# Hedgehog linear attention followed by a gated MLP: subtracting the mean inside the normalization instead of negating it first

## The chip, the core and the metric

The kernel runs on one core of one Trainium2 chip. A core has a matrix engine (TensorE, PE in the profile, with its weight loads as PEld), a vector engine (VectorE, DVE), a scalar engine (ScalarE, ACT), a general engine (GpSimd, POOL), and SyncE (SP), which here only issues transfers. Each engine works through its own list of instructions in order and waits on semaphores for the others. The metric is the device time of one execution in microseconds; the time of a kernel is the median of its runs.

## The reference

Two layers run one after the other on 8 batches of 576 positions. The first is an attention with a feature map; the second normalizes half of its hidden features, mixes them over the positions, and multiplies them with the other half. This is the part that the change touches:

```python
def _moe_ref(x, w_in, w_spatial, b_spatial, w_out):
    h = np.maximum(x @ w_in, 0.0)
    d_ff = h.shape[-1]
    u, v = (h[..., :d_ff // 2].copy(), h[..., d_ff // 2:].copy())
    mu = np.mean(v, axis=-1, keepdims=True)
    var = np.mean((v - mu) ** 2, axis=-1, keepdims=True)
    v_n = (v - mu) / np.sqrt(var + 1e-06)
    v_s = np.einsum('ts,bsd->btd', w_spatial, v_n) + b_spatial[None, :, None]
    gated = u * v_s
    return (gated @ w_out).astype(np.float32)
```

Here x is the output of the attention, (8, 576, 512), w_in is 512 x 1024, so u and v have 512 features for each position, w_spatial is 576 x 576 and w_out 512 x 512.

## The kernel before

The order of all work is written out by hand in one long string, ORDER. Each word of it names an operation, its batch and chunk, the PSUM banks or buffers that it takes, and, after an @, the engine (A for ACT, V for DVE, P for POOL, S for SP). Operations of different batches and of the two layers are interleaved there, so that the second layer of one batch runs beside the first layer of later batches. An engine never takes its instructions in another order than the string's: an instruction that waits holds up everything behind it on its engine.

The 576 positions of a batch are four chunks of 128 positions (c = 0 to 3), and a tail of 64. The tails of two batches share the 128 partitions of one tile, so tails go by pairs of batches (g = 0 to 3).

The path of v in the second layer is this, for a chunk of 128 positions by 512 features:

- vm (L964): four matmuls on PE give x times the v half of w_in in a PSUM bank.
- vr: ACT or DVE applies the relu and writes the tile vr, bf16. There are five buffers vr, so a later vr waits until an older one has been read.
- vb and va (L986, L990): DVE gathers mean and variance into mv, a tile that holds the pairs (mean, variance) of two chunks.
- vw (function root): POOL turns two chunks' variances into reciprocal roots in rs. This is done with an addition of 1e-6, a negation of the means in mv, and a power of -0.5.
- vn (function normalize, on POOL): one tensor_scalar with two operations and two scalars per partition, over 128 x 512 elements in bf16, writes the normalized chunk into the tile vn.
- sm (L1046 and L1048 on PE): each output bank takes four matmuls over the four chunks of vn and one over the tail vnt. So the first sm of a batch needs all four vn and the tail.
- sg (L1055 on DVE) multiplies with u, om (L1061 on PE) multiplies with w_out.

The tails have the same steps under the names vmt, vrt, vbt, vat, vwt, vnt and smt (L1113 and L1115 for the matmuls). Where both batches of a pair are done at once, vnt issues two instructions of 64 x 512.

POOL has more to do than this: it scales v by the features' weights in the first layer (vs, vst, L637 and L649), which the matmuls kv (L667, L669) read, divides by the attention's denominator (x, L813), splits the maxima in two bf16 halves (mhl, L682 and L683), and issues some of the loads. All of it stands in the same queue as root and normalize.

In the functions below, [:, :, 0] of mv is the mean and [:, :, 1] the variance; ENG[e] is the engine that the word of ORDER names, which is POOL for every vn and vnt.

Of the kernel before, what the change touches and what calls it, by code (L numbers as in the profile page):

```python
# [11 lines left out]
ALU = mybir.AluOpType  # L12
# [156 lines left out]
def kernel(  # L169
# [16 lines left out]
    nc = tc.nc  # L186
# [47 lines left out]
        mv=([P, 2, 2], FP32),  # L234
        rs=([P, 2, 1], FP32),
# [41 lines left out]
    ENG = dict(A=nc.scalar, V=nc.vector, P=nc.gpsimd, S=nc.sync)  # L277
# [689 lines left out]

    def root(rs, mv, r=slice(0, P)):
        nc.gpsimd.tensor_scalar(out=mv[:, :, 1], in0=mv[:, :, 1], scalar1=1e-6, scalar2=1.0, op0=ALU.add, op1=ALU.mult)
        nc.gpsimd.tensor_scalar(out=mv[:, :, 0], in0=mv[:, :, 0], scalar1=-1.0, scalar2=0.0, op0=ALU.mult, op1=ALU.add)  # L970
        nc.gpsimd.tensor_tensor(out=rs, in0=mv[:, :, 1], in1=neghalf[r, 0:rs.shape[1]], op=ALU.pow)

    def normalize(e, out_, in_, mv, rs):
        ENG[e].tensor_scalar(out=out_, in0=in_, scalar1=mv, scalar2=rs, op0=ALU.add, op1=ALU.mult)  # L974

    @op
    def vm(e, b, c):
# [14 lines left out]
    @op  # L992
    def vw(e, b, cc):
        root(get("rs", (b, cc)).rearrange("p n o -> p (n o)"), at["mv", (b, cc)])

    @op
    def vn(e, b, c):
        cc, y = c // 2, c % 2
        normalize(e, get("vn", b)[:, c, 0:HALF], at["vr", (b, c)], at["mv", (b, cc)][:, y, 0:1], at["rs", (b, cc)][:, y, :])
# [17 lines left out]
    @op  # L1017
    def vwt(e, g, i):
        root(get("rs", ("t", g, i))[rows[i], 0, :], at["mv", ("t", g, i)][rows[i], 0:1, :], rows[i])

    @op
    def vnt(e, g, i):
        for bl in parts[i]:
            r = rows[bl]
            normalize(e, get("vnt", g)[r, bl, :], at["vr", ("t", g, i)][r], at["mv", ("t", g, i)][r, 0, 0:1],
                      at["rs", ("t", g, i)][r, 0, :])
# [114 lines left out]
    with tc.manual_schedule():  # L1141
        for word in ORDER.split():
            word, _, e = word.partition("@")
# [35 lines left out]
```

## Time and profile before

| what | value |
|---|---|
| time, median of 3 runs | 258.3 us (257.01 to 259.43) |
| span of the profiled execution, first to last instruction | 253.3 us |
| median less the span | 5.0 us |
| busy: PE / DVE / ACT / POOL | 242.0 / 216.3 / 202.6 / 194.3 us |
| normalizing instructions (L974) on POOL | 40, 24.4 + 6.2 us busy |
| negations (L970) on POOL | 21, 4.1 us busy |
| granted TensorE clock over the span | 1.000 |

The profile is of one execution. The page does not list that execution's own total time; its span is 253.3 us, and the 5.0 us between span and median stand for what lies around it. Groups of instructions are given as their line, engine, operation, tiles and shapes, then the number of instructions, busy microseconds, mean nanoseconds of one, and how long the engine idled ahead of them and for whom. In the timeline a row is one instruction, or several alike, with its start, its length from the first start to the last end, and the idle time ahead in square brackets. A few matmul records are missing from the trace, so a group of four can read x3.

### The profile page before, as it was taken

Reading aid. Unit: us, or ns where it says so; the run is one execution under the profiler, and the core shown is the slowest. Engines: PE = TensorE matmul, PEld = TensorE weight load, DVE = VectorE, ACT = ScalarE, POOL = GpSimd, SP = SyncE. Lnnn points to the kernel's source line nnn. Section 1 sums busy time; section 2 is a strip of 40 time slices with the busy share of each in tenths; the row PEclk is TensorE's granted clock in tenths of the full one; section 3 lists DMA queues with packets and bytes.
Section 4 is the critical chain, followed back from the end, with each engine's and each line's share of the span. In section 5 each row is a group of like instructions: output and inputs, shape, how many; then the busy total and the mean of one; then the engine's idle time right before and its main releaser. Section 6 shows DMA issues by size and latency. Waiting matters only on the chain.

```text
span 253.3 us, 8099 instructions
## 1 busy us (share of the span) xinstructions
PE 242.0 (96%) x3254; PEld 155.5 (61%) x3291; DVE 216.3 (85%) x374; ACT 202.6 (80%) x344; POOL 194.3 (77%) x312
## 2 busy tenths in 40 slices
PE   7999989999999999898999999999999999999993
PEld 7888778656656666665565576556446765644542
DVE  1899989999999978999999999999998979657540
ACT  4899889999989999999999999889989702434222
POOL 8369997999698898589989996999899833495400
PEclk9999999999999999999999999999999999999999
DMA  7999995999899998999999969897730260521145
GB/s 197 304 184 254 234 245 91 195 145 126 165 282 113 122 265 131 208 225 154 171 180 256 196 149 207 89 256 183 228 113 15 44 123 6 208 44 41 52 113 208
DMA packets 80089, 41.33 MB, mean 163 GB/s; under 512 B 48946, under 2 KB 75442, under 8 KB 80052
## 3 DMA queue, kind: packets, MB, share of 16 engines
q1 hardware_dynamic: 58772, 30.06, 50.7%
q0 software_dynamic: 20592, 10.10, 32.3%
q10 hardware_dynamic: 688, 0.66, 0.8%
q8 instruction: 25, 0.41, 0.7%
q14 instruction: 12, 0.10, 0.1%
HBM read 32.82 MB, written 9.44 MB: 167 GB/s over the span
## 4 chain that ended last, share of the span: by engine, by line
PE 73%; DMA 7%; POOL 6%; DVE 6%; ACT 4%; issue 3%; SPq 0%; POOLq 0%; DVEq 0%
PE banks L1032 11%; PE banks L964 10%; PE banks L1061 10%; PE banks L1046 9%; PE banks L582 5%; DMA ld<-in_q_dram 5%; PE banks L667 4%; PE banks L790 3%; PE banks L369 3%; DMA xT<-x 2%; PE banks L513 2%; POOL vs L637 2%; PE banks L762 2%; PE banks L1048 2%; DVE mq L587 2%
## 5 line engine op out<-in xcount | busy, mean ns | idle before, releaser
L712 ACT ACTIVATE qf<-banks 128x1024 bf16<-128x1024 f32 x72 | 70.8, 1033 | 2.1 <-PE banks L697 0.7
L637 POOL TENSOR_TENSOR vs<-v,em 128x512 bf16<-128x512 f32 x64 | 65.6, 1043 | 2.5 <-PE banks L697 1.8
L591 ACT ACTIVATE kf<-banks 128x1024 bf16<-128x1024 f32 x64 | 63.3, 1037 | 2.7 <-PE banks L582 1.9
L587 DVE TENSOR_REDUCE mq<-banks 128x8 f32<-128x1024 f32 x36 | 43.2, 1214 | 1.4 <-PE banks L582 0.9
L587 DVE TENSOR_REDUCE mk<-banks 128x8 f32<-128x1024 f32 x32 | 38.6, 1215 | 1.6 <-PE banks L582 1.5
L1032 PE MATMUL banks<-xT,w_u 128*128 128x512 bf16 x128 | 32.3, 379 | 0.4 <-DVE mq L587 0.3
L1046 PE MATMUL banks<-w_spT,vn 128*128 128x512 bf16 x117 | 31.8, 379 | 0.5
L964 PE MATMUL banks<-w_v,xT 128*128 128x512 bf16 x115 | 30.4, 379 | 1.3 <-DMA xT<-x 0.5
L1061 PE MATMUL banks<-w_out,uT 128*128 128x512 bf16 x115 | 29.4, 379 | 0.6 <-issue 0.2
L1055 DVE TENSOR_TENSOR uT<-banks,uT 128x512 bf16<-128x512 f32 x32 | 21.7, 682 | 6.4 <-PE banks L1048 3.8
L281 ACT COPY ob<-banks 128x512 f32<-128x512 f32 (+1 forms) x24 | 14.0, 582 | 15.9 <-PE banks L1061 13.5
L813 POOL TENSOR_TENSOR x<-tq,rc 128x512 bf16<-128x512 f32 x16 | 16.7, 1044 | 12.7 <-DVE rc L810 9.6
L974 POOL TENSOR_SCALAR vn<-vr,mv,rs 128x512 bf16<-128x512 bf16 x32 | 24.4, 769 | 1.2
L986 DVE BATCH_NORM_STATS2 st<-vr 128x6 f32<-128x512 bf16 x32 | 21.5, 680 | 3.6 <-ACT vr L287 3.3
L667 PEld LDWEIGHTS <-kf 128*128 128x128 bf16 x512 | 21.9, 97 | 4.3 <-issue 0.4
L667 PE MATMUL banks<-vs,kf 128*128 128x66 bf16 x512 | 24.4, 194 | 0.0
L582 PE MATMUL banks<-wphi,T 64*128 64x128 bf16 x512 | 22.9, 217 | 0.4 <-ACT uT L287 0.3
L669 PE MATMUL banks<-vst,kft 128*128 128x66 bf16 x128 | 21.2, 192 | 0.0
L582 PEld LDWEIGHTS <-T 64*128 64x128 bf16 x512 | 15.9, 94 | 8.4 <-issue 6.4
L1032 PEld LDWEIGHTS <-w_u 128*128 128x128 bf16 x128 | 11.4, 97 | 12.8 <-issue 1.2
L287 ACT ACTIVATE vr<-banks 128x512 bf16<-128x512 f32 (+1 forms) x23 | 13.7, 604 | 6.1 <-POOL vnt L974 3.4
L1046 PEld LDWEIGHTS <-vn 128*128 128x128 bf16 x128 | 11.4, 97 | 11.5
(137 smaller groups left out, 512.1 us busy)
## 6 DMA issues: line engine op xcount, KB each, us to landing
v<-in_v_dram SPq DMA_DIRECT2D x16, 512.0 KB, 6.1
out_dram<-ob SPq DMA_DIRECT2D x31, 256.0 KB, 2.7
ld<-in_k_dram POOLq DMA_DIRECT2D x7, 512.0 KB, 8.8
ld<-in_q_dram POOLq DMA_DIRECT2D x7, 512.0 KB, 8.1
out_dram<-ob SPq DMA_DIRECT2D x9, 128.0 KB, 4.7
uT<-in_q_dram SPq DMA_DIRECT2D x2, 512.0 KB, 6.3
vt<-in_v_dram SPq DMA_DIRECT2D x8, 128.0 KB, 3.3
vn<-in_moe_w_spatial_dram POOLq DMA_DIRECT2D x1, 576.0 KB, 8.1
```

The costliest lines, as they stand in the source:

```text
L582: nc.tensor.matmul(out=bank(banks[y])[:, n * F:(n + 1) * F], lhsT=xT[halves[y], n, :], rhs=wphi[halves[y], :], start=True, stop=True)
L587: nc.vector.tensor_reduce(out=out_, in_=pp.rearrange("p y (n f) -> p y n f", f=F), axis=AX.X, op=ALU.max, apply_absolute_value=True)
L591: nc.scalar.activation(out=kf[:, s].rearrange("p y n f -> p y (n f)"), in_=pp, func=AF.Exp, bias=0.0, scale=(1.0, -1.0)[s])
L637: ENG[e].tensor_tensor(out=get("vs", (b, j))[:, s, :, 0:D], in0=at["v", (b, j // 2)][:, (j % 2) * n:(j % 2 + 1) * n, :], in1=at["em", (b, ...
L667: nc.tensor.matmul(out=pv[:, hh, s, :], lhsT=kf[:, s, c % 2, 2 * hh + c // 2, :], rhs=w[:, s, NB * hh + c, :], start=(c == 0), stop=False)
L712: nc.scalar.activation(out=at["qf", u][:, s].rearrange("p y n t -> p y (n t)"), in_=at["pq", u], func=AF.Exp, bias=0.0, scale=(1.0, -1.0)[s])
L964: nc.tensor.matmul(out=bank(place)[r], lhsT=lhs[:, kc, r], rhs=w_v[:, kc, :], start=(kc == 0), stop=(kc == KC - 1))
L974: ENG[e].tensor_scalar(out=out_, in0=in_, scalar1=mv, scalar2=rs, op0=ALU.add, op1=ALU.mult)
L1032: nc.tensor.matmul(out=bank(place).rearrange("p (c t) -> p c t", c=NB), lhsT=w_u[:, kc, dc * P:(dc + 1) * P], rhs=at["xT", b][:, :, kc, :] ...
L1046: nc.tensor.matmul(out=bank(place), lhsT=at["vn", b][:, c, cs], rhs=w_spT[:, c, 0:T0], start=(c == 0), stop=False)
L1055: nc.vector.tensor_tensor(out=u, in0=at["psp", (b, dc)], in1=u, op=ALU.mult)
L1061: nc.tensor.matmul(out=bank(place), lhsT=at["uT", b][:, dc, c * P:(c + 1) * P], rhs=w_out[:, dc, :], start=(dc == 0), stop=(dc == KC - 1))
```

## The change

The function root no longer multiplies the means by -1, and normalize subtracts the mean as its first operation where it added the negated mean. Its second operation, the multiplication by rs, stays.

```diff
     def root(rs, mv, r=slice(0, P)):
         nc.gpsimd.tensor_scalar(out=mv[:, :, 1], in0=mv[:, :, 1], scalar1=1e-6, scalar2=1.0, op0=ALU.add, op1=ALU.mult)
-        nc.gpsimd.tensor_scalar(out=mv[:, :, 0], in0=mv[:, :, 0], scalar1=-1.0, scalar2=0.0, op0=ALU.mult, op1=ALU.add)
         nc.gpsimd.tensor_tensor(out=rs, in0=mv[:, :, 1], in1=neghalf[r, 0:rs.shape[1]], op=ALU.pow)
 
     def normalize(e, out_, in_, mv, rs):
-        ENG[e].tensor_scalar(out=out_, in0=in_, scalar1=mv, scalar2=rs, op0=ALU.add, op1=ALU.mult)
+        ENG[e].tensor_scalar(out=out_, in0=in_, scalar1=mv, scalar2=rs, op0=ALU.subtract, op1=ALU.mult)
```

ORDER is the same, and the lists of the other engines are the same but for the line numbers behind L970, which are one lower. On POOL, 21 rows go. This is the place in POOL's list where the first batch is normalized for the first time: mv_150 holds two chunks' means and variances, rs_156 their reciprocal roots.

```order
 L969 TENSOR_SCALAR mv_150<-mv_150 128x2
-L970 TENSOR_SCALAR mv_150<-mv_150 128x2
-L971 TENSOR_TENSOR rs_156<-mv_150,neghalf 128x2
+L970 TENSOR_TENSOR rs_156<-mv_150,neghalf 128x2
 L402 DMA ld_62<-in_k_dram 128x8x256
```

Between the addition (L969) and the power (L971 before, L970 now) nothing is left. In the second batch the same piece, with the numbers of the buffers and the semaphores that an instruction waits for in brackets (Pool is POOL's own), reads:

```order
 L969 TENSOR_SCALAR mv_5_155<-mv_5_155 128x2 [waits DVE_49]
-L970 TENSOR_SCALAR mv_5_155<-mv_5_155 128x2
-L971 TENSOR_TENSOR rs_4_160<-mv_5_155,neghalf_179 128x2 [waits Pool_49]
-L974 TENSOR_SCALAR vn_2_163<-vr_2_143,mv_5_155,rs_4_160 128x512 [waits Pool_49]
+L970 TENSOR_TENSOR rs_4_160<-mv_5_155,neghalf_179 128x2 [waits Pool_49]
+L973 TENSOR_SCALAR vn_2_163<-vr_2_143,mv_5_155,rs_4_160 128x512 [waits Pool_49]
```

The power waits for POOL's own addition in both, and the normalization waits for the power; the negation had waited for nothing. The normalizations keep their places, tiles and shapes; only their first operation differs, which the rows do not show.

## Prediction

> **What bounds the kernel now.** I read the page first, for the busy shares of the engines.
>
> ```profile
> span 253.3 us, 8099 instructions
> PE 242.0 (96%) x3254; PEld 155.5 (61%) x3291; DVE 216.3 (85%) x374; ACT 202.6 (80%) x344; POOL 194.3 (77%) x312
> POOL 8369997999698898589989996999899833495400
> ```
>
> PE is busy for 96% of the span, so the kernel ends when PE's list ends, and a change counts by the idle time that it puts into PE or takes out. Only 11.3 us (253.3 less 242.0) could be taken out at all. POOL's row in 40 slices of 6.3 us says that its 77% is an average: between slice 8 and slice 32 it is mostly at 8 or 9 tenths. What POOL does later there, it does later for everything behind it.
>
> Then the groups of POOL's instructions, shapes kept apart, for what the touched instructions cost and for other instructions of the same size.
>
> ```profile
> L637 POOL TENSOR_TENSOR vs<-v,em 128x512 bf16<-128x512 f32 x64 | 65.6, 1043 | 2.5 <-PE banks L697 1.8 <-ACT em L596 0.2
> L974 POOL TENSOR_SCALAR vn<-vr,mv,rs 128x512 bf16<-128x512 bf16 x32 | 24.4, 769 | 1.2
> L974 POOL TENSOR_SCALAR vnt<-vr,mv,rs 64x512 bf16<-64x512 bf16 x8 | 6.2, 769 | 0.4
> L971 POOL TENSOR_TENSOR rs<-mv,neghalf 128x2 f32<-128x2 f32 x16 | 11.2, 701 | 0.0
> L683 POOL TENSOR_TENSOR mhl<-mq,mhl 128x8 bf16<-128x8 f32 x19 | 3.8, 202 | 1.6
> L970 POOL TENSOR_SCALAR mv<-mv 128x2 f32<-128x2 f32 x16 | 3.1, 193 | 1.3
> L969 POOL TENSOR_SCALAR mv<-mv 128x2 f32<-128x2 f32 x16 | 3.1, 193 | 5.8 <-DVE mv L990 4.8
> L337 POOL TENSOR_SCALAR sel<-sel 128x512 bf16<-128x512 bf16 x1 | 1.5, 1517 | 0.0
> L283 POOL COPY vnt<-ident 128x512 bf16<-128x512 bf16 x2 | 1.2, 612 | 0.0
> ```
>
> The time of an instruction on POOL depends on the arithmetic as well as on the size: a power over 2 elements per partition (L971) takes 701 ns, a subtraction over 8 (L683) 202 ns. And two tensor_scalar instructions of one size and type differ by a factor of two: L974, an addition followed by a multiplication, takes 769 ns; L337, which multiplies by -1 with no second operation, takes 1517 ns.
>
> Last the timeline, at the places where normalized chunks are handed to PE: the last normalizations of each of the eight batches on POOL, and the matmuls that read them.
>
> ```profile
> 60.08 3.02 POOL L974 TENSOR_SCALAR vn<-vr,mv,rs 128x512 bf16<-128x512 bf16 x4
> 63.09 0.76 POOL L974 TENSOR_SCALAR vnt<-vr,mv,rs 64x512 bf16<-64x512 bf16 x1
> 86.59 2.28 POOL L974 TENSOR_SCALAR vn<-vr,mv,rs 128x512 bf16<-128x512 bf16 x3
> 131.35 1.63 POOL L974 TENSOR_SCALAR vnt<-vr,mv,rs 64x512 bf16<-64x512 bf16 x2
> 141.64 1.53 POOL L974 TENSOR_SCALAR vn<-vr,mv,rs 128x512 bf16<-128x512 bf16 x2
> 180.26 1.63 POOL L974 TENSOR_SCALAR vnt<-vr,mv,rs 64x512 bf16<-64x512 bf16 x2
> 191.96 1.53 POOL L974 TENSOR_SCALAR vn<-vr,mv,rs 128x512 bf16<-128x512 bf16 x2
> 228.41 0.77 POOL L974 TENSOR_SCALAR vn<-vr,mv,rs 128x512 bf16<-128x512 bf16 x1
> 234.43 3.03 POOL L974 TENSOR_SCALAR vn<-vr,mv,rs 128x512 bf16<-128x512 bf16 x4
> ...
> 64.89 0.38 PE L1048 MATMUL banks<-w_spT,vnt 128*128 128x512 bf16 x1
> 88.72 1.02 PE L1046 MATMUL banks<-w_spT,vn 128*128 128x512 bf16 x3
> 133.46 0.38 PE L1048 MATMUL banks<-w_spT,vnt 128*128 128x512 bf16 x1
> 146.05 0.28 PE L1113 MATMUL banks<-w_spT,vn 128*128 128x64 bf16 x4
> 182.86 0.38 PE L1048 MATMUL banks<-w_spT,vnt 128*128 128x512 bf16 x1
> 193.74 0.81 PE L1046 MATMUL banks<-w_spT,vn 128*128 128x512 bf16 x3
> 229.70 0.81 PE L1046 MATMUL banks<-w_spT,vn 128*128 128x512 bf16 x3
> 238.91 0.28 PE L1113 MATMUL banks<-w_spT,vn 128*128 128x64 bf16 x4
> ```
>
> POOL's end (start plus length) against PE's start gives the slack of each hand-over: batch 0, 64.89 - 63.85 = 1.04 us; batch 1, the last chunk is read by the last matmul of the group, which starts at 88.72 + 1.02 - 0.38 = 89.36, so 89.36 - 88.87 = 0.5; batch 2, 133.46 - 132.98 = 0.5; batch 3, 146.05 - 143.17 = 2.9; batch 4, 182.86 - 181.89 = 1.0; batch 5, 193.74 - 193.49 = 0.25; batch 6, 229.70 - 229.18 = 0.5; batch 7, 238.91 - 237.46 = 1.45. PE does not wait for POOL here, but in six of eight batches it arrives within about 1 us of it.
>
> **The change part by part.** The first part takes 21 negations out of POOL's list. Starts tell what each holds up; the rows of the first root, and a pair beside it whose second instruction waits for the first:
>
> ```profile
> 55.19 0.19 POOL L969 TENSOR_SCALAR mv<-mv 128x2 f32<-128x2 f32 x1
> 55.46 0.19 POOL L970 TENSOR_SCALAR mv<-mv 128x2 f32<-128x2 f32 x1
> 55.62 0.73 POOL L971 TENSOR_TENSOR rs<-mv,neghalf 128x2 f32<-128x2 f32 x1
> 57.31 0.21 POOL L682 CAST mhl<-mq 128x8 bf16<-128x8 f32 x1
> 57.60 0.20 POOL L683 TENSOR_TENSOR mhl<-mq,mhl 128x8 bf16<-128x8 f32 x1
> ```
>
> From the addition's start to the power's start are now 55.62 - 55.19 = 0.43 us. With the negation gone the power follows the addition whose result it needs; the row of that kind nearest by is L682 to L683, 0.29 us, and L969 to L970 is 0.27. I take 0.27, so a root gets 0.16 us shorter, and the 21 together 3.4 us. The Trainium skill (Perfetto Trace Analysis, GPSIMD Engine Instruction) says that a GpSimd instruction's recorded span is unreliable and should be replaced by the spacing of starts; by that rule the trace agrees, since L970's span is 0.19 us where the next start comes 0.16 us later. By spans the sum would be 21 x 0.193 = 4.1 us instead.
>
> The second part changes the first operation of 40 normalizations (32 vn, 8 vnt) from an addition to a subtraction. The trace shows no tensor_scalar on POOL that subtracts, so its price is bounded by the rows of the same size. Below stands the COPY with 612 ns, a pass without arithmetic; the price of an addition, 769, lies just above. L637, two tensors read, takes 1043. L337 takes 1517 with one operation; if a second operation cost as much again beyond the 193 ns that a small tensor_scalar takes (L970), that would be 1517 + 1324 = 2841 ns. I take 1517 ns. Every tensor_scalar on POOL that is an addition and a multiplication, in either order, belongs to the cheap kind as far as its size lets one see (L974, 769; L969 and L970 are too small to tell); the only one that is something else, L337, costs double. Its input is one column repeated, but so is that of the COPY, which is the faster of all, so the reading is not what makes it slow. A subtraction with a multiplication is something else as well; that it shares L337's price is my choice.
>
> At 1517 ns a normalization takes e = 0.748 us longer. On POOL this is 40 x 0.748 - 3.4 = +26.5 us, of 194.3. What PE sees is worked out batch by batch: normalizations times e, less roots times 0.16, plus what POOL still lags from before, less POOL's idle ahead, less the slack above. After a hand-over that stalls PE, the schedule as a whole is later, and POOL lags it by the slack; where POOL then idles, that lag goes.
>
> - Batch 0: 5 normalizations, 3 roots: 3.74 - 0.48 = 3.26, less 1.04: PE stalls 2.2 us.
> - Batch 1: its tail and first chunk with their roots add 1.18, of which POOL's idle of 0.34 takes some; one root and three chunks add 2.08; 2.92 less 0.5: 2.4.
> - Batch 2: three chunks and two roots add 1.92, an idle of 0.80 takes some; one root, a chunk and two tails add 2.08; 3.2 less 0.5: 2.7.
> - Batch 3: 4 normalizations, 2 roots: 2.67, with a lag of 0.5, less 2.9: 0.3.
> - Batch 4: 6 normalizations, 3 roots: 4.0, less 1.0: 3.0.
> - Batch 5: 2.67, a lag of 1.0 less an idle of 0.29, less 0.25: 3.1.
> - Batch 6: the first chunk is lost in an idle of 2.50; 5 normalizations, 2 roots: 3.4, less 0.5: 2.9.
> - Batch 7: 2.67, less 1.45: 1.2.
>
> The idle times are these:
>
> ```profile
> 85.36 0.19 POOL L969 TENSOR_SCALAR mv<-mv 128x2 f32<-128x2 f32 x1 [0.34 <-DVE mv L990]
> 127.58 0.19 POOL L969 TENSOR_SCALAR mv<-mv 128x1 f32<-128x1 f32 x1 [0.80 <-DVE mv L1015]
> 182.19 0.19 POOL L969 TENSOR_SCALAR mv<-mv 128x2 f32<-128x2 f32 x1 [0.29 <-DVE mv L990]
> 221.73 1.04 POOL L813 TENSOR_TENSOR x<-tq,rc 128x512 bf16<-128x512 f32 x1 [2.50 <-DVE rc L810]
> ```
>
> The sum is 17.8 us. Against the profiled execution the span would be 253.3 + 17.8 = 271.1, and with the 5.0 us around it 276.1: the forecast is 276 us. What queues behind a slower normalization on POOL (vs, x, mhl, loads) is late by the same lag; I count it only through PE's stall, which is the weak point of the sum: where the chunk's slack is large, as in batch 3, a late vs or x may stall PE in its place. The Trainium skill (GPSIMD Engine Reference, Performance pitfalls for Q7 kernels) has a dependent chain of fp32 operations at 4 cycles an element unless it is unrolled; at the 1.2 GHz that the page gives, an estimate from it for 512 elements is 1.71 us, and the same eight lines would give 25 us and 284. No row here shows cycles, and L974 with 769 ns is faster than such a chain.
>
> **The rivals.** The first is that a subtraction costs what an addition costs: then nothing but the negations changes. For it speaks L683, where a subtraction of two tensors takes 0.20 us beside the 0.21 us of the conversion L682 ahead of it; against it L337. The place is L974 at 769 ns, and the point from which it decides is a price below about 0.85 us, where 40 x 0.08 = 3.2 us undo the 3.4 us of the roots. PE waits nowhere for a normalization now, so it gains little; at most the 0.16 us of one to three roots in the three tightest batches, some 0.5 us, gives 257.8 us, not slower. The lower bound of 612 ns would take another 6.3 us off POOL, and no more than 1.5 us off PE: 256.5. [...]
>
> The second is that both operations are priced like L337's one, 2841 ns. Then e is 2.07, POOL's work is 40 x 2.07 - 3.4 = 79 us more, 274 us in all, and POOL becomes the bound: the eight lines give 8.8, 9.0, 10.6, 5.6, 10.9, 8.4, 9.5 and 6.5, together 69 us, and 328 us.
>
> The third is a mild price, that of L637, 1043 ns: e is 0.274, batches 0, 3 and 7 hide theirs, and 0.2, 0.2, 0.2, 1.2 and 0.5 remain: 2.3 us, and 260.6.
>
> **How the numbers follow.** I give the forecast, a price from 1.25 to 2.1 us, 0.47; the same price as an addition 0.28; the mild price 0.10; a price above 2.1 us 0.15. The forecast's own range is 267 (1.25 us: 8 us by the same lines) to 300 us (2.1 us: 41 us). The range of 8 in 10 has to take in the first rival, which reaches from 256.5 to 259, and leaves out the prices above 2.1 us and a few hundredths below 257: 257 to 300. A measurement of this kernel can tell about 1%, 2.6 us, from no change. Faster by more than that is left only to the lower bound, 0.04; within 1% are the rest of the first rival and half of the mild price, 0.28; slower is 0.68.
>
> **What would show it.** In the profile of the changed kernel the normalization's group (line 973) shows the price at once: near 1500 ns for the forecast, 769 for the first rival, near 2800 for the second. The start of the power should come 0.27 us after the addition's. If the price is near 1500 ns, PE should idle ahead of L1045 and L1047 (before L1046 and L1048) for 2 to 3 us in batches 0, 1, 2, 4, 5 and 6 and hardly in batch 3. The prediction is wrong in its price if the group reads otherwise, and in its sum if the group reads 1500 ns and the time is not within some 5 us of 276: then POOL's lag reached PE through vs and x, or was lost in idle time that I counted as fixed.

## The result, and the profile after

The changed kernel takes 304.7 us (median of 6 runs, 303.2 to 306.3) against 256.5 us for the kernel before in the same comparison: a ratio of 1.188 (95% interval 1.184 to 1.193). That is 48 us slower, where 18 us slower and 276 us were forecast, and it lies above the range of 257 to 300.

The page of the changed kernel, its busy shares and the chain that ended last:

```profile
span 301.6 us, 8078 instructions
PE 255.9 (85%) x3254; PEld 159.6 (53%) x3291; DVE 217.6 (72%) x374; ACT 203.4 (67%) x344; POOL 243.2 (81%) x291
POOL 48%; PE 28%; DVE 9%; issue 6%; DMA 5%; POOLq 1%; ACT 1%; SPq 0%; DVEq 0%
```

The span grew by 48.3 us, POOL's busy time by 48.9 us (194.3 to 243.2). POOL now makes up 48% of the chain, with PE at 28%. PE, which was busy for 96% of the span, is busy for 85%; and its own busy time grew by 13.9 us though it has the same matmuls: its mean granted clock was 0.949 in this execution, against 1.000 before.

POOL's groups, shapes kept apart, and the longest waits for POOL:

```profile
L973 POOL TENSOR_SCALAR vn<-vr,mv,rs 128x512 bf16<-128x512 bf16 x32 | 66.2, 2074 | 1.2
L973 POOL TENSOR_SCALAR vnt<-vr,mv,rs 64x512 bf16<-64x512 bf16 x8 | 16.6, 2073 | 0.4
L970 POOL TENSOR_TENSOR rs<-mv,neghalf 128x2 f32<-128x2 f32 x16 | 11.4, 714 | 1.3
L337 POOL TENSOR_SCALAR sel<-sel 128x512 bf16<-128x512 bf16 x1 | 1.5, 1522 | 0.0
...
PE banks L1045 <- POOL vn L973: 16.7, 6, 5.8
DVE tq L802 <- POOL x L813: 11.7, 5, 4.2
```

A normalization takes 2074 ns where it took 769: 40 x 1.305 = 52 us more. L337 is where it was. PE, which waited nowhere for a normalization before, waits 16.7 us for them ahead of L1045 (and 4.0 us ahead of L1047 and L1112), and DVE waits 11.7 us for the division x, which stands in the same queue.

The first root in the timeline:

```profile
54.95 0.19 POOL L969 TENSOR_SCALAR mv<-mv 128x2 f32<-128x2 f32 x1
55.23 0.73 POOL L970 TENSOR_TENSOR rs<-mv,neghalf 128x2 f32<-128x2 f32 x1
```

From the addition to the power are 0.28 us, 0.27 by the prediction, against 0.43 before. So the part that removes the negations did on POOL what was expected.

For each batch, the first matmul that reads its normalized tail (sm, or smt for batches 3 and 7), in the trace of before and then of after:

```profile
64.89 0.38 PE L1048 MATMUL banks<-w_spT,vnt 128*128 128x512 bf16 x1
89.58 0.38 PE L1048 MATMUL banks<-w_spT,vnt 128*128 128x512 bf16 x1
146.16 0.19 PE L1115 MATMUL banks<-w_spT,vnt 128*128 128x64 bf16 x1
194.39 0.38 PE L1048 MATMUL banks<-w_spT,vnt 128*128 128x512 bf16 x1
230.56 0.38 PE L1048 MATMUL banks<-w_spT,vnt 128*128 128x512 bf16 x1
239.03 0.19 PE L1115 MATMUL banks<-w_spT,vnt 128*128 128x64 bf16 x1
```

```profile
69.76 0.61 PE L1047 MATMUL banks<-w_spT,vnt 128*128 128x512 bf16 x1 [0.59 <-POOL vnt L973]
100.99 0.63 PE L1047 MATMUL banks<-w_spT,vnt 128*128 128x512 bf16 x1
151.32 0.39 PE L1047 MATMUL banks<-w_spT,vnt 128*128 128x512 bf16 x1 [1.24 <-POOL vnt L973]
168.46 0.19 PE L1114 MATMUL banks<-w_spT,vnt 128*128 128x64 bf16 x1
212.47 0.63 PE L1047 MATMUL banks<-w_spT,vnt 128*128 128x512 bf16 x1
231.98 0.63 PE L1047 MATMUL banks<-w_spT,vnt 128*128 128x512 bf16 x1
276.58 0.63 PE L1047 MATMUL banks<-w_spT,vnt 128*128 128x512 bf16 x1 [0.22 <-issue]
287.31 0.19 PE L1114 MATMUL banks<-w_spT,vnt 128*128 128x64 bf16 x1
```

(Batches 2 and 4 of before, at 133.46 and 182.86, stand in the prediction.) The difference at a batch, less the difference at the batch before it, is the delay that the batch adds. Beside it stands what the eight lines of the prediction give with the measured price, e = 2.074 - 0.769 = 1.305 us, in place of 0.748:

| batch | 0 | 1 | 2 | 3 | 4 | 5 | 6 | 7 | sum |
|---|---|---|---|---|---|---|---|---|---|
| lines, at 2.07 us | 5.0 | 5.2 | 6.1 | 2.5 | 6.4 | 5.4 | 5.7 | 3.5 | 39.8 |
| after | 4.9 | 6.5 | 6.4 | 4.4 | 7.3 | 8.0 | 8.4 | 2.3 | 48.3 |

(The lines' entries are rounded; unrounded they sum to 39.6.) The first batch is on the line; from then on every batch but the last adds 0.3 to 2.7 us more. Another thing in these rows: in five of eight the matmul is recorded with 0.61 to 0.63 us where 0.38 is usual.

So two questions were left: why a subtraction costs 2.07 us and not 1.52, and where the 8.7 us beyond the lines come from.

### The profile page after: what moved, and what is told of

The parts are those of the page before. It is cut to its first block, busy times and chain, and to the rows that moved or that the text cites. A ratio compares the mean times of both kernels' runs of the same rounds, so it can differ in the third digit from the quotient of the medians.

```text
span 301.6 us, 8078 instructions
## 1 busy us (share of the span) xinstructions
PE 255.9 (85%) x3254; PEld 159.6 (53%) x3291; DVE 217.6 (72%) x374; ACT 203.4 (67%) x344; POOL 243.2 (81%) x291
## 4 chain that ended last, share of the span: by engine, by line
POOL 48%; PE 28%; DVE 9%; issue 6%; DMA 5%; POOLq 1%; ACT 1%; SPq 0%; DVEq 0%
POOL vn L973 19%; POOL vs L637 8%; PE banks L1045 6%; POOL vnt L973 5%; POOL rs L970 5%; DMA ld<-in_q_dram 4%; PE banks L369 3%; POOL x L813 2%; PE banks L1060 2%; PE banks L582 2%; PE banks L513 2%; DVE mq L587 2%; PE banks L667 2%; POOL vst L649 2%; DVE tq L802 2%
## 5 line engine op out<-in xcount | busy, mean ns | idle before, releaser
L973 POOL TENSOR_SCALAR vn<-vr,mv,rs 128x512 bf16<-128x512 bf16 x32 | 66.2, 2074 | 1.2
L1045 PE MATMUL banks<-w_spT,vn 128*128 128x512 bf16 x117 | 38.7, 443 | 20.2 <-POOL vn L973 16.7
L1045 PEld LDWEIGHTS <-vn 128*128 128x128 bf16 x128 | 12.5, 108 | 35.3 <-POOL vn L973 18.2
L813 POOL TENSOR_TENSOR x<-tq,rc 128x512 bf16<-128x512 f32 x16 | 16.7, 1043 | 13.9 <-DVE rc L810 11.0
L802 DVE TENSOR_TENSOR tq<-banks,wq 128x528 f32<-128x528 f32 x17 | 12.0, 704 | 16.7 <-POOL x L813 11.7
L287 ACT ACTIVATE uT<-banks 128x512 bf16<-128x512 f32 x23 | 13.8, 609 | 15.1 <-PE banks L1031 14.9
## 6 DMA issues: line engine op xcount, KB each, us to landing
out_dram<-ob SPq DMA_DIRECT2D x31, 256.0 KB, 2.7
```

Source lines behind the costliest of these rows:

```text
L287: nc.scalar.activation(out=out_, in_=in_, func=AF.Relu, bias=0.0, scale=1.0)
L1045: nc.tensor.matmul(out=bank(place), lhsT=at["vn", b][:, c, cs], rhs=w_spT[:, c, 0:T0], start=(c == 0), stop=False)
```

## The experiments

### Prices of eleven pairs of operations

```diff
+        scr = [buf["vr"][3], buf["xt"][0].rearrange("p h d -> p (h d)")]
+        vin, m1, r1 = at["vr", (7, 3)], at["mv", (7, 1)][:, 1, 0:1], at["rs", (7, 1)][:, 1, :]
+        pairs = [(ALU.add, ALU.mult), (ALU.subtract, ALU.mult), (ALU.mult, ALU.add), (ALU.mult, ALU.subtract),
+                 (ALU.add, ALU.add), (ALU.subtract, ALU.add), (ALU.mult, ALU.mult), (ALU.max, ALU.mult),
+                 (ALU.add, None), (ALU.subtract, None), (ALU.mult, None)]
+        for i, (a, c) in enumerate(pairs):
+            nc.gpsimd.tensor_scalar(out=scr[i % 2], in0=vin, scalar1=m1, scalar2=None if c is None else r1, op0=a,
+                                    **({} if c is None else dict(op1=c)))
```

> The kernel before, with eleven more tensor_scalar instructions on GpSimd behind its last one, all over the same 128 x 512 bf16 tile with the same two scalars per partition, one for each pair of operations: add-mult, subtract-mult, mult-add, mult-subtract, add-add, subtract-add, mult-mult, max-mult, and add, subtract and mult alone. Their results go nowhere. Theory (the price hangs on the pair of operations, a few pairs being cheap): add-mult 770 ns, subtract-mult 2070 ns, mult alone about 1520 ns, mult-add cheap as well. Rival (the price hangs on the place or on contention in the changed kernel): subtract-mult 770 ns here, where nothing else runs on GpSimd.

The timeline of POOL behind its last normalization, in the order of the list in the diff:

```profile
238.08 0.78 POOL L1156 TENSOR_SCALAR vr<-vr,mv,rs 128x512 bf16<-128x512 bf16 x1
238.83 2.10 POOL L1156 TENSOR_SCALAR xt<-vr,mv,rs 128x512 bf16<-128x512 bf16 x1
240.91 0.78 POOL L1156 TENSOR_SCALAR vr<-vr,mv,rs 128x512 bf16<-128x512 bf16 x1
241.66 2.10 POOL L1156 TENSOR_SCALAR xt<-vr,mv,rs 128x512 bf16<-128x512 bf16 x1
243.73 2.11 POOL L1156 TENSOR_SCALAR vr<-vr,mv,rs 128x512 bf16<-128x512 bf16 x1
245.81 2.10 POOL L1156 TENSOR_SCALAR xt<-vr,mv,rs 128x512 bf16<-128x512 bf16 x1
247.87 0.79 POOL L1156 TENSOR_SCALAR vr<-vr,mv,rs 128x512 bf16<-128x512 bf16 x1
248.62 2.11 POOL L1156 TENSOR_SCALAR xt<-vr,mv,rs 128x512 bf16<-128x512 bf16 x1
250.69 1.59 POOL L1156 TENSOR_SCALAR vr<-vr,mv 128x512 bf16<-128x512 bf16 x1
252.24 1.59 POOL L1156 TENSOR_SCALAR xt<-vr,mv 128x512 bf16<-128x512 bf16 x1
253.78 1.59 POOL L1156 TENSOR_SCALAR vr<-vr,mv 128x512 bf16<-128x512 bf16 x1
```

Add-mult, mult-add and mult-mult take 0.78 to 0.79 us. Subtract-mult, mult-subtract, add-add, subtract-add and max-mult take 2.10 to 2.11 us, and each operation alone, addition and multiplication among them, takes 1.59 us. So the price hangs on the pair as a whole, not on the subtraction: an addition after an addition is as dear. The results go to the tiles xt and vr in turn; a single operation takes 1.59 us into either. Nothing else runs on POOL here, and DVE is idle from 246.3 to 250.3 us while the prices stay the same, so contention is not the reason.

### Sizes, fixed numbers, and VectorE

```diff
+        for a, c, n in [(ALU.add, ALU.mult, 128), (ALU.add, ALU.mult, 256), (ALU.subtract, ALU.mult, 128),
+                        (ALU.subtract, ALU.mult, 256)]:
+            nc.gpsimd.tensor_scalar(out=scr[0][:, 0:n], in0=vin[:, 0:n], scalar1=m1, scalar2=r1, op0=a, op1=c)
+        for a, c in [(ALU.add, ALU.mult), (ALU.subtract, ALU.mult)]:
+            nc.gpsimd.tensor_scalar(out=scr[0], in0=vin, scalar1=0.5, scalar2=2.0, op0=a, op1=c)
...
+            nc.vector.tensor_scalar(out=scr[1], in0=vin, scalar1=0.5, scalar2=2.0, op0=a, op1=c)
...
+            nc.vector.tensor_scalar(out=scr[1], in0=vin, scalar1=m1, scalar2=r1, op0=a, op1=c)
```

> The kernel before, with more instructions behind GpSimd's last one. On GpSimd: add-mult and subtract-mult over 128 and 256 columns, then both over 512 columns with fixed numbers in place of the scalars per partition. On VectorE: both pairs over 512 columns, with fixed numbers and with scalars per partition. Theory (a slow path of GpSimd for every pair but a few, with a price per element): from 2.07 us at 512 columns and some 0.2 us fixed, subtract-mult takes 0.67 us at 128 and 1.14 us at 256 columns, add-mult 0.34 and 0.48; fixed numbers change nothing; VectorE takes the same time for both pairs. Rival (a fixed price of 1.3 us for each slow instruction, code that has to be found): subtract-mult 1.6 us at 128 columns.

Each line's own durations (least, median and greatest, in ns), and the two sizes of the first line apart:

```profile
L1155 POOL TENSOR_SCALAR vr<-vr,mv,rs x4: 462/684/1222, 237.6 to 239.7; 128x128 bf16<-128x128 bf16 x2, 128x256 bf16<-128x256 bf16 x2
L1157 POOL TENSOR_SCALAR vr<-vr x2: 619/1272/1924, 241.0 to 241.7; 128x512 bf16<-128x512 bf16 x2
L1161 DVE TENSOR_SCALAR xt<-vr,mv,rs x2: 412/412/412, 250.8 to 251.3; 128x512 bf16<-128x512 bf16 x2
...
L1155 POOL TENSOR_SCALAR vr<-vr,mv,rs 128x256 bf16<-128x256 bf16 x2 | 1.8, 890 | 0.2
L1155 POOL TENSOR_SCALAR vr<-vr,mv,rs 128x128 bf16<-128x128 bf16 x2 | 1.3, 636 | 0.1
```

The pairs of means give add-mult 462 and 558 ns at 128 and 256 columns, and subtract-mult 810 and 1222 ns. With 769 and 2074 at 512 columns, add-mult grows by 0.75 to 0.82 ns a column, subtract-mult by 3.2 to 3.3, from the same fixed part of some 0.4 us. The rival of a fixed price falls. The expected 0.34, 0.48, 0.67 and 1.14 us were all some 0.1 us low, since the fixed part had been taken from small instructions without scalars per partition; fixed numbers save 0.15 us for either pair (0.62 and 1.92 us), which had been expected to change nothing. On VectorE both pairs take 412 ns: the price belongs to GpSimd.

### The two parts of the change alone

```diff
-        nc.gpsimd.tensor_scalar(out=mv[:, :, 0], in0=mv[:, :, 0], scalar1=-1.0, scalar2=0.0, op0=ALU.mult, op1=ALU.add)
```

> The first part of the change alone: the 21 negations go, the normalization keeps its addition. (It then adds the mean where it should subtract it.) Theory: GpSimd's list gets 21 x 0.16 = 3.4 us shorter, PE waits nowhere for it, so the time stays within 1 us of the kernel before, 256 to 257 us. Rival (the root's power now stalls behind the addition): 21 x 0.1 us or more of lost time, 258 us or more.

Measured: 255.98 us, a ratio of 0.995 (0.991 to 0.999). The change without its dear pair of operations is a small gain, 1.3 us (0.2 to 2.4), where no more than 1 us was expected; the rival's loss of time behind the addition did not come.

```diff
-        ENG[e].tensor_scalar(out=out_, in0=in_, scalar1=mv, scalar2=rs, op0=ALU.add, op1=ALU.mult)
+        ENG[e].tensor_scalar(out=out_, in0=in_, scalar1=mv, scalar2=rs, op0=ALU.subtract, op1=ALU.mult)
```

> The second part of the change alone: the normalization subtracts, and the 21 negations stay. (It then adds the mean.) Theory (GpSimd's list now sets the time at nearly every hand-over): the negations cost all of their 21 x 0.16 = 3.4 us, so 3 to 4 us more than the changed kernel, about 308 us. Rival (they are hidden as in the kernel before): within 1 us of the changed kernel, 304 to 305.5 us.

Measured: 307.3 us, a ratio of 1.199 (1.195 to 1.204), 2.6 us more than the changed kernel. So the second part makes the whole loss. By the intervals of the two ratios the 2.6 us are uncertain by some 1.6 us. So the rival's 1 us is unlikely, and most of POOL's list is on the path now, as the theory has it; whether all of it is, 2.6 against 3.4 us, cannot be told.

### The forecast's own price

```diff
-        ENG[e].tensor_scalar(out=out_, in0=in_, scalar1=mv, scalar2=rs, op0=ALU.add, op1=ALU.mult)
+        ENG[e].tensor_scalar(out=out_, in0=in_, scalar1=rs, scalar2=None, op0=ALU.mult)
```

(This is against the kernel before; the negation L970 goes as well.)

> The normalization at the forecast's own price: no negation, and one multiplication by rs with no second operation. (The mean is not subtracted at all.) Price expected 1520 ns. The eight lines of the prediction give 17.8 us, so 256.5 + 17.8 = 274 us. If the lines miss something that grows with the stalls, as the 48 us of the changed kernel against 40 by the lines at 2.07 us suggest, 276 to 280 us.

Measured: 281.7 us, a ratio of 1.094 (1.087 to 1.102), more than either expectation, with this group:

```profile
L973 POOL TENSOR_SCALAR vn<-vr,rs 128x512 bf16<-128x512 bf16 x32 | 49.9, 1568 | 1.1
```

At 1568 ns, e is 0.80 us and the lines give 19.9 us. Measured are 24 us (0.094 x 257.3), again some 4 us more. So the lines are short by about a fifth of what is measured at both prices: what they lack grows with the stalls.

### The clock behind the stalls

The matmuls of 0.61 us after a wait pointed to TensorE's clock. This was tried by keeping PE busy while it waits:

```diff
-sm.0.0:0
+warm.60:0 sm.0.0:0
-sm.1.0:3
+warm.45:3 sm.1.0:3
-sm.4.2:5
+warm.45:5 sm.4.2:5
-sm.5.1:2
+warm.45:2 sm.5.1:2
-sm.6.0:5
+warm.90:5 sm.6.0:5
```

> The changed kernel with small matmuls on the identity put ahead of the first sm of batches 0, 1, 4, 5 and 6 (60, 45, 45, 45, 90 of them, into the bank that this sm fills next), so that PE is busy for most of the time in which it waits for the normalization. Their results are overwritten. Theory (the stalls of 3 us and more bring a lower clock behind them, which is the part of the 48 us that the lines lack): the mean granted clock goes from 0.95 to 0.98 or more and the time falls by 4 to 9 us, to 296 to 301 us. Rival (the rest is lag that reaches PE through vs, x and their buffers): the time stays at 304 us or grows.

Measured: 300.75 us, a ratio of 1.167 (1.158 to 1.176), a mean granted clock of 0.971: 4 us less than the changed kernel, at the end of what was expected, with a clock below the 0.98 expected. At batch 4 this kernel was 31.8 us behind the kernel before, where the changed one was 29.6 (its first tail matmul starts at 214.68 against 212.47). There the small matmuls filled no wait:

```profile
208.63 4.96 PE L369 MATMUL banks<-ident 128*128 128x128 bf16 x45 [2.98 <-ACT vr L287]
```

They write the bank that ACT's relu vr has to empty first, and this vr had itself waited 3.40 us for POOL to read an older tile vr. So they start only after the wait of 2.98 us. The granted clock was 1.00 up to 206 us and 0.50 from 208 us on, and the 45 took 4.96 us, where they take 2.67 at batch 1 below. (In the changed kernel the first sm of batch 4 waits 2.97 us for the same vr, a path from POOL to PE that the lines do not have.) They were left out there in the next run:

> The changed kernel with the small matmuls ahead of the first sm of batches 0, 1, 5 and 6 only (60, 45, 45, 90); those ahead of batch 4 are left out, since the run with five places lost some 6 us there. Theory (the lower clock behind long stalls is a good part of what the lines lack): mean granted clock 0.98 or more, 294 to 299 us. Rival (the gain of the first such run was chance, or lost again at the next hand-over, because GpSimd's list sets the time): 301 us or more.

Measured: 298.85 us, a ratio of 1.165 (1.160 to 1.171), granted clock 0.980 against 0.949. The 5.9 us less (uncertain by some 1.8 us) came as the theory expected. They are what the small matmuls save, not all that the lower clock costs, for the clock is not back at 1.000. At batch 1 it is seen best. These are windows of 11 us around its hand-over, in the changed kernel and then in this one, and the window around batch 2's in the changed kernel; after the busy times of the engines stands the granted clock:

```profile
96.00:107.00 11.00, 7.66 (x69) 4.11 (x72) 3.71 (x8) 4.40 (x10) 8.92 (x10) 0.69 0.43 104
```

```profile
94.00:105.00 11.00, 9.55 (x135) 6.31 (x134) 5.65 (x11) 6.47 (x13) 10.68 (x11) 1.00 0.39 98
```

```profile
150.00:165.00 15.00, 11.65 (x141) 6.47 (x143) 10.63 (x20) 11.81 (x23) 14.27 (x14) 1.00 1.17 204
```

And the matmuls at batch 1 without and with the small ones ahead:

```profile
98.53 0.61 PE L1045 MATMUL banks<-w_spT,vn 128*128 128x512 bf16 x1 [2.70 <-POOL vn L973]
101.41 1.91 PE L1045 MATMUL banks<-w_spT,vn 128*128 128x512 bf16 x4
```

```profile
93.66 2.67 PE L369 MATMUL banks<-ident 128*128 128x128 bf16 x45
99.05 1.03 PE L1045 MATMUL banks<-w_spT,vn 128*128 128x512 bf16 x4
```

In the changed kernel the granted clock is 1.00 up to 98.0 us and 0.50 from 98.25 to 104.75 us. The first matmul after 2.70 us without work takes 0.61 us, and four later ones take 1.91; with 45 small ones put into that wait the four take 1.03. Around batch 2, whose waits for normalizations are 1.24 us and less and where the longest other wait is 1.84 us, the clock stays full. The Trainium skill (TensorE: Matmul & The Clock Gate, Part 1) says that TensorE falls to half its clock after about 3.4 us of idleness and needs as long a stretch of work to come back; the trace agrees in kind, with a granted clock of 0.50 and 0.61 us for 0.38, but here 2.70 us of idleness were enough.

### The division that stands behind the normalizations

DVE waits 11.7 us for x in the changed kernel. In batch 3 the divisions of batch 4's attention stand between the normalizations on POOL; they were moved to DVE:

```diff
-qu.4.1.0:0@P
+qu.4.1.0:0@V
```

(and the three others of batch 4 alike)

> The changed kernel with the four divisions of batch 4's attention (x, L813), which stand among batch 3's normalizations, on VectorE in place of GpSimd. Theory (in batch 3 the lag reaches PE through x: VectorE waits for x before it can fill the one buffer tq again, and PE for VectorE): the delay that batch 3 adds falls from 4.4 to about 2.5 us, and the whole time by 3 to 6 us with the 4 x 1.04 us that GpSimd is spared. Rival (x is late but not what PE waits for): the delay of batch 3 stays at 4 us or more, and the time falls by less than 2 us.

Measured: 301.7 us, a ratio of 1.179 (1.173 to 1.184), 3.0 us less than the changed kernel, uncertain by some 1.8. The hand-overs of batches 2 and 3, and DVE's wait:

```profile
150.13 0.39 PE L1047 MATMUL banks<-w_spT,vnt 128*128 128x512 bf16 x1 [1.24 <-POOL vnt L973]
165.35 0.19 PE L1114 MATMUL banks<-w_spT,vnt 128*128 128x64 bf16 x1
...
DVE tq L802 <- POOL x L813: 3.3, 2, 2.5
```

They are now 16.7 and 19.2 us behind the kernel before, so batch 3 adds 2.5 us where it added 4.4. (The changed kernel was 17.9 and 22.3 us behind; the 1.2 us at batch 2 lie ahead of what was moved.) The 2.5 us are the number that the theory gave, but not by its path. These are the tails of batch 2 and the last chunks of batch 3 on POOL, and the matmul that waits for them, in the changed kernel and then in this one:

```profile
149.20 4.23 POOL L973 TENSOR_SCALAR vnt<-vr,mv,rs 64x512 bf16<-64x512 bf16 x2
164.22 4.14 POOL L973 TENSOR_SCALAR vn<-vr,mv,rs 128x512 bf16<-128x512 bf16 x2
168.42 0.20 PE L1112 MATMUL banks<-w_spT,vn 128*128 128x64 bf16 x1 [1.34 <-POOL vn L973]
```

```profile
148.01 4.24 POOL L973 TENSOR_SCALAR vnt<-vr,mv,rs 64x512 bf16<-64x512 bf16 x2
161.12 4.14 POOL L973 TENSOR_SCALAR vn<-vr,mv,rs 128x512 bf16<-128x512 bf16 x2
165.31 0.20 PE L1112 MATMUL banks<-w_spT,vn 128*128 128x64 bf16 x1 [1.83 <-POOL vn L973]
```

In both, POOL works without a gap from the tails to the last chunk, and PE waits for POOL at the end. From the end of the one to the end of the other POOL takes 14.9 us (153.43 to 168.36), and 13.0 us without two divisions of 1.04 us that stood there. That is the 1.9 us. PE no longer waits for tq ahead of this hand-over, but its wait for POOL grew from 1.34 to 1.83 us. So the gain of batch 3 is POOL's shorter list, and that a late x holds up PE is not shown.

What the line of batch 3 had too small is its lag of 0.5 us. The first tail matmul of batch 2 needs only the first of the two tail normalizations: it starts at 151.32 us, when POOL has 2.1 us of the second still to go, where POOL had been done 0.5 us ahead of it in the kernel before. That is a lag of 2.6 us. The line of batch 2 counts the second normalization too, so what one line has too little the other has too much. In the run with four places, where the clock stays at 1.00 in between, the two batches add 8.6 us (their first tail matmuls start at 146.89 and 164.04 us), and the two lines give 8.6.

### Both remedies together

> The changed kernel with both remedies: the small matmuls ahead of the first sm of batches 0, 1, 5 and 6, and the four divisions x of batch 4 on VectorE. Theory (the 8 to 9 us that the eight lines lack are the lower clock and the late x, two separate causes): the gains add, 5.7 + 3 = 8 to 9 us, so a ratio to the kernel before of about 1.155 and 295 to 297 us; what is left over the kernel before is then the 39.6 us of the lines at the measured price. Rival (both shorten the same waits): no more than 6 to 7 us together, 298 us or more.

(Its edit is that of the four places and that of the four divisions.) Measured: 295.9 us, a ratio of 1.152 (1.146 to 1.158): 8.8 us less than the changed kernel, and 39.1 us over the kernel before, where the lines give 39.6. The two gains add (5.9 and 3.0). That this leaves the size of the lines is in part chance: the divisions spared are POOL's own work, which the lines do not count as added, and the granted clock is still 0.974 to 0.994. By batches the agreement is looser than in the sum: from its first tail matmuls (70.31, 99.29, 147.33, 162.54, 207.62, 226.53, 269.23 and 280.55 us) the batches add 5.4, 4.3, 4.2, 2.5, 8.4, 7.4, 6.5 and 2.9 us, 41.5 in this trace. Batches 1 and 2 add less than their lines, batches 4 and 5 2 us more. No run looked into those two.

### A cheap pair for L337

```diff
-                             scalar2=None, op0=ALU.mult)
+                             scalar2=1.0, op0=ALU.mult, op1=ALU.mult)
```

> The kernel before with one thing changed: the single multiplication L337, which makes the tile sel in the first 25 us, gets a second one by 1.0, so that it is a mult-mult pair. Theory from the prices: 1.52 us become 0.77 or less. Whether the time follows depends on what waits for sel on the way into the first features: between 0 and 0.75 us less, 255.7 to 256.5 us, more likely no difference that can be told.

```profile
L337 POOL TENSOR_SCALAR sel<-sel 128x512 bf16<-128x512 bf16 x1 | 0.6, 615 | 0.0
```

The instruction went from 1517 to 615 ns by a second operation that does nothing. The time did not follow: 256.0 us, a ratio of 0.998 (0.994 to 1.002). No version beat the kernel before by more than the negation's 1.3 us, and a way to leave the negation out with a cheap pair and the right sign was not found.

## Why the prediction was wrong

**The place, the sign and the mechanism were right.** POOL's price for the normalization decided, PE came to wait for it at the hand-overs, and the part with the negations was worth little, 1.3 us.

**The step that failed is the price.** The prediction wrote that a subtraction with a multiplication "shares L337's price" and took 1517 ns, measured on one operation. Measured are 2074 ns for two: a dear second operation costs 0.5 us more (2.10 against 1.59 us). That was between the value taken and the second rival's 2841 ns, which had priced a second operation at 1.32 us. In the eight lines it makes 39.6 us of 17.8, and so 21.8 us of the miss. L337's price as a sign of the dear kind was read rightly: its input (four columns, each repeated, and not one as the prediction has it) was not the cause, since its time fell to 615 ns with the same input and a cheap pair.

**The lines lacked another 8.7 us, explained in part.** The lower clock behind stalls of 2.7 us and more makes about 5.9 us of it, by the run with four places; the prediction counted a stall with its length and nothing behind it. The other 2.8 us stay open. The weak point that the prediction named, a late x, is not shown to be the cause: moving the four divisions saves 3.0 us, but in batch 3 by POOL's shorter list. The lag of 0.5 us in batch 3 was 2.6, with as much too much in batch 2, which leaves the sum as it is. In the run with four places what is left stands mostly in batches 4 and 5, which add 15.7 us where their lines give 11.8. The miss of 28.7 us (304.7 less 276) is then 21.8 + 8.7, less 1.8 for the kernel before, which was 258.3 us in the first runs and 256.5 in this comparison. At 1568 ns, near the price of the forecast, the run took 281.7 us, 5.7 from 276, where the prediction's own sign allowed some 5: its sum was a little short even at its own price.

**The range** ended at 300 for a price of 2.1 us, nearly the one measured. What put the result outside it is the part beyond the lines; only the price had been given two ends.

**The smaller steps.** 0.27 us from addition to power: 0.28. The first rival's gain from the negations of up to 0.5 us: 1.3 us, with an interval from 0.2 to 2.4. That batch 3 would hardly stall: it added 4.4 us, by the lag above. Three small sums are off and nothing hangs on them: 257.8 less 1.5 is 256.3 and not 256.5, and the shares for within 1% and slower add up to 0.29 and 0.67. The estimate of 1.71 us from the Trainium skill (GPSIMD Engine Reference, Performance pitfalls for Q7 kernels) left out the fixed part. With the 0.4 us of the run with sizes it would be an estimate of 2.11 us, near the measured 2.07 to 2.10, and its 3.33 ns an element lie near the measured 3.2 to 3.3 ns a column; no run shows whether a dependent chain is what makes these pairs dear.

## What to carry to other kernels

On GpSimd, choose the pair of operations of a tensor_scalar by its measured price; a sign that can be put elsewhere for 0.16 us may be worth 1.3 us at each use. When an instruction gets slower on an engine that hands work to TensorE just in time, sum its length over the hand-overs, less the slack of each, and then add for the clock behind each stall of some 3 us. See in the timeline which instruction a hand-over really waits for: where the first of two normalizations is enough, the second belongs to the next hand-over. Other work in the slow queue is on the path too, and may be moved. A price read off one row of another form needs both of its ends carried through the whole sum, and so does the sum itself.

## What the runs showed of the hardware that was not expected

- A tensor_scalar on GpSimd over 128 x 512 bf16 takes 0.78 us for add-mult, mult-add and mult-mult, 2.10 us for the other five pairs tried, and 1.59 us for a single operation: a multiplication becomes faster with a second one by 1.0 (1517 to 615 ns, with fixed numbers).
- On GpSimd subtract-mult costs 3.2 to 3.3 ns a column and add-mult 0.75 to 0.82, from the same fixed part of some 0.4 us; scalars per partition cost either pair 0.15 us more than fixed numbers. VectorE takes 412 ns for either pair.
- Within 2.70 us of idleness TensorE's granted clock fell from 1.00 to 0.50 and stayed there for some 6.5 us (0.69 on average over the 11 us around it); waits of 1.24 and 1.84 us left it at 1.00.
